# A recurrent attention block with a SwiGLU layer behind it: every engine's order from a list schedule computed in the kernel, fixed tiles, one PSUM pair per role, and the output product accumulated over d_ff

## The chip, the cores and the metric

The kernel runs on one core of a Trainium2 chip. The metric is device time in microseconds (us) of one execution, median of the runs. All matrices are fp32.

## The reference, cut to what matters

```python
for t in range(S):                       # B=4, H=8, S=768, D=40; state is B x H x D x D
    y[:, :, t] = einsum('bhd,bhde->bhe', r_t, state)
    Sa = einsum('bhde,bhe->bhd', state, a_t)
    state = state * w_t[:, :, None, :] - outer(Sa, b_t) + outer(v_t, k_t)
x = y.transpose(0, 2, 1, 3).reshape(3072, 320)
xn = x / sqrt(mean(x * x) + 1e-6) * rms_g
g, val = xn @ w_gate, xn @ w_val         # 320 x 1536 each
out = (g * sigmoid(g) * val) @ w_out     # 1536 x 320
```

The weights `moe_w_gate`, `moe_w_val` and `moe_w_out` arrive as 64-bit floats and are turned into fp32 in the kernel.

## The kernel before, in words

**Chunks.** The 768 steps are cut into 24 chunks of `C = 32`. In each chunk all 32 pairs of batch and head are worked on together, on 128 partitions. A chunk has four parts.

- `front(c)`: loads w, a, k and b of the chunk (`wan`, `kbn`), transposes them (`twa`, `tkb`), and goes through five levels (1, 2, 4, 8, 16). Each level is a Gram product of 32 small matmuls (`gram`), a masked copy of it into `LT` on VectorE (`copy_predicated`, L214), eight transposes (`nat`), a ScalarE copy of these into `KN`, and new `K` and `A`. At the end `LT` goes to DRAM (`sB`) and comes back, spread over the partitions, as `M`.
- `inverse(c)`: 31 pairs of VectorE instructions (`tmp`, L261, and `Yi`, L262), each of which needs the one before; the first needs `M`. The result returns through DRAM (`sY`) into `LT`.
- `crit(c)`: the recurrence over chunks. Matmuls `X` (from `LT`, `VU` and the state `ST`), `U` (needs the inverse), `up`, then the new `ST`; `state()` transposes it (`S`).
- `off(c)`: the chunk's output: transposes of `VU` (`tvu`), `score`, its masked copies `As`, the products `y` (one with the state, five levels), their sums on VectorE, `xn`, the norm, and the transposes `tx` into `xg`.

**Feed-forward.** `feed(g)` works on two chunks (256 rows). For six pairs of 128 columns of d_ff it loads `wf` (320 KB per 128 columns), runs 12 matmuls `h`, then `sg` (a sigmoid on ScalarE) and two VectorE products into `hT`, a tile that holds all 1536 columns. After all of them it loads `wo` twelve times and runs the 24 matmuls `po`. `narrow` turns the weights into fp32 in 48 pieces at the start, with loads and stores on GpSimd's queue.

**What sets the order.** A scheduler outside the kernel orders the instructions by priorities; `together` gives `crit` and `off` a high priority, `feed` raises its three instructions behind `h` by less. Tiles come out of rotating pools, and PSUM is four double banks, `C` for the recurrence, `O` for the output, `B` for `front` and `F` for `feed`.

**Names in the profile.** All matmuls but the transposes stand under L81, the transposes `turned` under L179, all of SP's DMA under L84. Each fp32 matmul appears as two records, a transpose as one.

Of the kernel before, what the change touches and what calls it, by code (L numbers as in the profile page):

```python
# [19 lines left out]
CG = 2  # L20
EPS = 1e-6


@with_exitstack
def kernel(
# [47 lines left out]
    dram = ctx.enter_context(tc.tile_pool(name="dram", bufs=3, space=DRAM))  # L73
    dram1 = ctx.enter_context(tc.tile_pool(name="dram1", bufs=1, space=DRAM))
# [3 lines left out]
    sW = [dram1.tile([P, WF], FP32, name=f"sW{f}") for f in range(FT)]  # L78

    def mm(o, lhsT, rhs, start=True, stop=True):  # L80
        nc.tensor.matmul(o, lhsT, rhs, start=start, stop=stop, skip_group_check=True)  # L81

    def dma(o, i, by=nc.sync):
        by.dma_start(out=o, in_=i)  # L84

    MUL, ADD, SUB = ALU.mult, ALU.add, ALU.subtract
    TT = nc.vector.tensor_tensor
# [8 lines left out]
    def everything():  # L96
        with ExitStack() as st:
            const = st.enter_context(tc.tile_pool(name="const", bufs=1))
            one = st.enter_context(tc.tile_pool(name="one", bufs=1))
            two = st.enter_context(tc.tile_pool(name="two", bufs=2))  # L100
            three = st.enter_context(tc.tile_pool(name="three", bufs=3))
            eight = st.enter_context(tc.tile_pool(name="wf", bufs=4))
            psum = {t: st.enter_context(tc.tile_pool(name="ps" + t, bufs=1, space=PSUM)) for t in "COBF"}

            def dbl(name, tag):
                return psum[tag].tile([P, 2, 512], FP32, name=name, tag=tag)


            ident = const.tile([P, P], FP32, name="ident")
            nc.gpsimd.memset(ident, 0.0)  # L110
            nc.gpsimd.affine_select(ident, ident, pattern=[[-1, P]], channel_multiplier=1, base=0,
                                    compare_op=ALU.not_equal, fill=1.0)

            iw = const.tile([P, 3, C], I32, name="iw")
            nc.gpsimd.iota(iw[:, 0], pattern=[[0, C]], base=0, channel_multiplier=1)
            nc.gpsimd.iota(iw[:, 1], pattern=[[1, C]], base=0, channel_multiplier=0)
            nc.vector.tensor_scalar(iw[:, 0], iw[:, 0], C - 1, None, ALU.bitwise_and)
            TT(iw[:, 0], iw[:, 0], iw[:, 1], ALU.bitwise_xor)
            msk = const.tile([P, len(LEVELS), C], FP32, name="msk")
            for j, l in enumerate(LEVELS):  # L120
                nc.vector.tensor_scalar(iw[:, 2], iw[:, 0], j, None, ALU.logical_shift_right)
                nc.vector.tensor_scalar(msk[:, j], iw[:, 2], 1.0, None, ALU.is_equal)

            mhalf = const.tile([P, 1], FP32, name="mhalf")
            nc.gpsimd.memset(mhalf, -0.5)
            gcol = const.tile([P, KT], FP32, name="gcol")
            for p0, kt, src in ((0, 0, 0), (0, 1, P), (0, 2, 2 * P), (64, 2, 2 * P)):
                m = min(P, DM - src)
                nc.gpsimd.dma_start(out=gcol[p0:p0 + m, kt:kt + 1],
                                    in_=moe_rms_g[src:src + m].rearrange("(d o) -> d o", o=1))  # L130

            eye = const.tile([P, C // 4, C], FP32, name="eye")
            nc.gpsimd.memset(eye, 0.0)
            for m in range(4):
                e = eye[m * BH:(m + 1) * BH]
                nc.gpsimd.affine_select(e, e, pattern=[[-4, C // 4], [1, C]], channel_multiplier=0, base=-m,
                                        compare_op=ALU.not_equal, fill=1.0)


            def keep(shape, name):  # L140
                t = const.tile(shape, FP32, name=name)
                nc.gpsimd.memset(t, 0.0)  # L142
                return t

            kbn_ = [keep([P, N, 2, 64], f"kbn{i}") for i in range(3)]
            wan = keep([P, N, 2, 64], "wan")
            rn = keep([P, N, 2, 64], "rn")
            r2n = keep([P, N, 2, 64], "r2n")
            LT_ = [keep([P, NI, C], f"LT{i}") for i in range(2)]
            VU_ = [keep([P, N, 2, 64], f"VU{i}") for i in range(2)]  # L150
            ST_ = [keep([P, N, 2, 64], f"ST{i}") for i in range(2)]
            nat5 = lambda t: t.rearrange("p n o e -> p (n o) e")

            Z = {}

            def tokens(t, i, x, src, tk):
                dma(nat5(t)[rows(i, x), :, 0:D], src[2 * i:2 * i + 2, :, tk, :].rearrange("q h s d -> s (q h) d"))

            def load(c, *what):
                tk = slice(c * C, (c + 1) * C)  # L160
                for i in range(2):
                    for nm in what:
                        t, x, src = {"k": (kbn_[c % 3], 0, k), "b": (kbn_[c % 3], 1, b), "w": (wan, 0, w),
                                     "a": (wan, 1, a), "v": (VU_[c % 2], 0, v)}[nm]
                        tokens(t, i, x, src, tk)

            def load_r(c):
                tk = slice(c * C, (c + 2) * C)
                for i in range(2):
                    dma(nat5(rn)[half(i), :, 0:D], r[2 * i:2 * i + 2, :, tk, :].rearrange("q h s d -> s (q h) d"))  # L170
                    rv = r[2 * i:2 * i + 2, :, tk, :].rearrange("q (m o) s d -> o s (q m) d", o=2)
                    for o in range(2):
                        dma(r2n[half(o), :, i, 0:D], rv[o])

            def turned(t, name, tag="B"):

                ps = dbl(name, tag).rearrange("p u f -> p (u f)").rearrange("p (n t) -> p n t", n=N)
                for n in range(N):
                    nc.tensor.transpose(ps[:, n, :], t[:, n].rearrange("p o e -> p (o e)"), ident)  # L179
                return ps  # L180

            def front(c):

                z = Z[c] = {}
                if c % 2 == 0:
                    z["rE"] = two.tile([P, N, 2, 2 * C], FP32, name="rE")
                    nc.scalar.copy(z["rE"].rearrange("p n i t -> p n (i t)"), turned(rn, "tr"))
                    z["r2"] = two.tile([P, N, 2, 2 * C], FP32, name="r2")
                    nc.scalar.copy(z["r2"].rearrange("p n o t -> p n (o t)"), turned(r2n, "tr2"))
                else:  # L190
                    z["rE"], z["r2"] = Z[c - 1]["rE"], Z[c - 1]["r2"]
                wa = turned(wan, "twa").rearrange("p n (i x t) -> p (n i) x t", i=2, x=2)
                T = two.tile([P, NI, 2 * C], FP32, name="T")
                z["T"] = Tl = {}
                o = 0
# [372 lines left out]
```

## Time and profile before

| | |
|---|---|
| median of 3 runs | 1994.24 us (1988.46 to 2005.21) |
| profiled execution: time / span | 1989.99 us / 1988.2 us |
| PE busy | 1683.9 us, 85% of the span |
| DVE, ACT, POOL busy | 957.0, 322.2, 299.8 us |
| DMA | 146.25 MB, mean 74 GB/s |
| mean granted TensorE clock | 0.780 |

How to read it: PE's busy time is the sum of records, and a record is longer when the granted clock is lower, so 85% busy does not mean 85% of what PE could do. PEclk in the row of slices is the clock that was granted, in tenths of full speed. The chain of waits names, from the last instruction back, what each step waited for.

### The profile page before, as it was taken

What the parts mean: (1) busy time and instruction counts of PE and PEld (TensorE: products, weight loads), DVE (VectorE), ACT (ScalarE), POOL (GpSimd) and SP (SyncE); (2) the same over time, 40 slices, a digit from 0 to 9 for tenths busy, and PEclk for the clock granted to TensorE, in tenths of its full rate; (3) what the DMA queues carried; (4) which work ended last, traced back from release to release, by engine and by line L of the source; (5) the groups of instructions that cost most, each with busy time, mean ns of one, the idle gap of its engine ahead of it and who ended that gap; (6) DMA issues with size and microseconds to landing.
All of it is one profiled execution on the core that took longest, in us unless ns stands there. A gap on an engine that the chain in (4) does not pass through costs nothing.

```text
span 1988.2 us, 66337 instructions
## 1 busy us (share of the span) xinstructions
PE 1683.9 (85%) x29640; PEld 1303.7 (66%) x29640; DVE 957.0 (48%) x3252; ACT 322.2 (16%) x518; POOL 299.8 (15%) x714
## 2 busy tenths in 40 slices
PE   1748968777899799998898998998998998989886
PEld 1647756666776577666676776776776776767554
DVE  3566566566542543553554525534544544653411
ACT  1111121121111111211211211111211111211100
POOL 4313222122010110110110101101101101110000
PEclk9995575665689877878867678688778688787889
DMA  4333232332333423323423233233233233222232
GB/s 79 70 77 87 68 84 63 79 78 57 101 80 95 84 52 82 79 47 79 87 54 75 62 70 85 60 66 96 66 73 78 60 74 80 62 59 67 66 93 63
DMA packets 309629, 146.25 MB, mean 74 GB/s; under 512 B 262304, under 2 KB 283808, under 8 KB 309344
## 3 DMA queue, kind: packets, MB, share of 16 engines
q1 hardware_dynamic: 303072, 124.31, 27.4%
q0 software_dynamic: 6272, 17.70, 3.1%
q8 instruction: 232, 3.80, 0.8%
q14 instruction: 53, 0.43, 0.1%
HBM read 125.83 MB, written 16.12 MB: 71 GB/s over the span
## 4 chain that ended last, share of the span: by engine, by line
PE 67%; DVE 13%; DMA 8%; issue 5%; ACT 3%; POOL 2%; SPq 1%; POOLq 0%; ACTq 0%; DVEq 0%
PE h L81 19%; PE y L81 11%; PE po L81 9%; PE nat L179 7%; PE gram L81 5%; PE X L81 4%; DMA M<-sB 3%; PE S L179 3%; DVE tmp L261 2%; DVE Yi L262 2%; DVE K L223 2%; PE U L81 2%; DMA rw<-in_moe_w_val_dram 1%; DVE LT L214 1%; PE score L81 1%
## 5 line engine op out<-in xcount | busy, mean ns | idle before, releaser
L81 PE MATMUL h<-xg,wf 128*128 128x256 f32 (+1 forms) x1728 | 506.8, 478 | 36.2 <-issue 19.5
L81 PEld LDWEIGHTS h<-xg,wf 128*128 128x128 f32 (+1 forms) x1728 | 307.1, 227 | 152.3 <-issue 111.7
L81 PE MATMUL po<-wo,hT 128*128 128x320 f32 x576 | 199.2, 492 | 32.8 <-DVE Yi L262 20.1
L81 PEld LDWEIGHTS gram<-A,K 40*64 40x64 f32 x7680 | 161.3, 163 | 98.8 <-issue 47.1
L179 PE MATMUL nat<-ident,K 128*128 128x128 f32 x960 | 190.8, 357 | 36.2 <-DVE LT L214 26.3
L81 PE MATMUL gram<-A,K 40*64 40x16 f32 x7680 | 175.1, 227 | 51.8 <-DVE tmp L261 17.8
L81 PEld LDWEIGHTS y<-As,KN 64*64 64x64 f32 x6144 | 167.6, 170 | 69.6 <-issue 50.3
L261 DVE TENSOR_TENSOR tmp<-Yi,M 128x60 f32<-128x60 f32 (+24 forms) x744 | 166.5, 224 | 93.4 <-DMA M<-sB 80.6
L81 PE MATMUL y<-As,KN 64*64 64x16 f32 x6144 | 193.2, 232 | 18.5 <-issue 14.8
L179 PEld LDWEIGHTS nat<-ident,K 128*128 128x128 f32 x960 | 149.6, 184 | 62.7 <-DVE LT L214 30.9
L262 DVE TENSOR_TENSOR Yi<-Yi,tmp 128x60 f32<-128x60 f32 (+24 forms) x744 | 169.1, 227 | 13.4
L81 PEld LDWEIGHTS po<-wo,hT 128*128 128x128 f32 x576 | 115.4, 214 | 82.5 <-issue 41.6
L246 ACT COPY KN<-nat 128x640 f32<-128x640 f32 x120 | 83.0, 692 | 463.0 <-PE nat L179 463.0
L224 POOL COPY K<-K 128x256 f32<-128x256 f32 x240 | 119.2, 523 | 202.4 <-PE nat L179 88.2
L223 DVE TENSOR_TENSOR K<-K,T 128x256 f32<-128x256 f32 x240 | 117.1, 497 | 39.3 <-PE nat L179 31.5
L433 DVE TENSOR_TENSOR sg<-h,sg 128x512 f32<-128x512 f32 x72 | 49.6, 689 | 168.6 <-ACT sg L432 168.3
L214 DVE COPY_PREDICATED LT<-msk,gram 128x256 f32<-128x256 uint32 x120 | 65.5, 546 | 133.2 <-PE gram L81 132.7
L245 POOL MEMSET KN<- 128x24 f32 x120 | 13.6, 117 | 592.7 <-PE y L81 365.1
L227 POOL COPY A<-A 128x256 f32<-128x256 f32 x120 | 57.7, 481 | 296.8 <-ACT A L201 117.8
L179 PE MATMUL S<-ident,ST 128*128 128x128 f32 x192 | 79.2, 427 | 18.2 <-POOL ST L142 15.2
L432 ACT ACTIVATE sg<-h 128x512 f32<-128x512 f32 x72 | 43.0, 598 | 284.2 <-PE h L81 271.5
L332 DVE TENSOR_TENSOR As<-score,msk 128x256 f32<-128x256 f32 x120 | 42.0, 417 | 65.9 <-PE score L81 65.9
(100 smaller groups left out, 1674.9 us busy)
## 6 DMA issues: line engine op xcount, KB each, us to landing
wf<-sW SPq DMA_DIRECT2D x144, 320.0 KB
wo<-sW SPq DMA_DIRECT2D x144, 160.0 KB
M<-sB SPq DMA_DIRECT2D x24, 512.0 KB
kbn<-in_k_dram SPq DMA_DIRECT2D x48, 80.0 KB
kbn<-in_b_dram SPq DMA_DIRECT2D x48, 80.0 KB
wan<-in_w_dram SPq DMA_DIRECT2D x48, 80.0 KB
wan<-in_a_dram SPq DMA_DIRECT2D x48, 80.0 KB
VU<-in_v_dram SPq DMA_DIRECT2D x48, 80.0 KB
```

The costliest lines, as they stand in the source:

```text
L81: nc.tensor.matmul(o, lhsT, rhs, start=start, stop=stop, skip_group_check=True)
L179: nc.tensor.transpose(ps[:, n, :], t[:, n].rearrange("p o e -> p (o e)"), ident)
L214: nc.vector.copy_predicated(side(LT, l, 1), side(msk, l, 1)[:, j:j + 1].bitcast(U32).to_broadcast((P, NI, G, l)), gr.rearrange("p o n t -> ...
L223: TT(side(K1[:, :, x], l, 0), side(K[:, :, x], l, 0), by[1], MUL)
L224: nc.gpsimd.tensor_copy(side(K1[:, :, x], l, 1), side(K[:, :, x], l, 1))
L227: nc.gpsimd.tensor_copy(side(A1, l, 0), side(A, l, 0))
L246: nc.scalar.copy(t[:, 0:NI * D].rearrange("p (n o e) -> p n o e", n=N, o=2), ps.rearrange("p n (o e) -> p n o e", o=2)[:, :, :, 0:D])
L261: TT(tmp, Y[:, 0:n, i:i + 1].to_broadcast((P, n, m)), M[:, i:i + 1, i + 1:].to_broadcast((P, n, m)), MUL)
L262: TT(Y[:, 0:n, i + 1:], Y[:, 0:n, i + 1:], tmp, SUB)
L332: TT(As[:, j].rearrange("p n (g l) -> p n g l", g=G), side(sc.rearrange("p o n t -> p (o n) t")[:, :, 0:C], l, 1), side(msk, l, 1)[:, j:j ...
L432: nc.scalar.activation(sg, h[:, 0], AF.Sigmoid)
L433: TT(sg, h[:, 0], sg, MUL)
```

## The change

The program is no longer issued as it is described. Each helper (`tt`, `ts`, `where`, `copy`, `scale`, `ptt`, `dma`, `pe`, ...) adds a piece to a `Plan`: the engine, a due time, an assumed duration, and the tiles that it reads and writes. At the end `Plan.issue` goes through all engines by a list schedule (at the earliest time at which some engine has a ready piece, that engine takes the ready piece that is due first) and issues the pieces in that order under `tc.manual_schedule()`, so that nothing reorders them.

```diff
+class Plan:
+    LATENCY = 0.1
...
+            t, e = best
+            i = min((i for i in waiting[e] if ready[i] <= t), key=lambda i: (self.pieces[i][1], i))
+            waiting[e].remove(i)
+            _, _, time, more, _ = self.pieces[i]
+            free[e] = t + time
+            order.append((t, i))
+            for j in users[i]:
+                ready[j] = max(ready[j], t + time + more + self.LATENCY)
...
+        for _, i in sorted(order):
+            self.pieces[i][4]()
...
+    def tt(due, o, a, b, op):
+        plan.add("DVE", due, 0.145 + 0.00104 * size(o), lambda: nc.vector.tensor_tensor(o, a, b, op), [o], [a, b])
+    def copy(due, o, a):
+        plan.add("ACT", due, 0.16 + 0.00083 * size(o), lambda: nc.scalar.copy(o, a), [o], [a])
+    def dma(due, o, i, by="SP"):
+        q, t = {"SP": (nc.sync, 0.06), "POOL": (nc.gpsimd, 1.0)}[by]
+        n = size(i) * list(i.ap)[0][1]
+        plan.add(by, due, t, lambda: q.dma_start(out=o, in_=i), [o], [i], 2.2 + n * 4 / 200e3)
...
+    ps_ = {t: Turns(n, [P, 2, 512], "ps" + t, pool=psum) for t, n in (("C", 1), ("B", 1), ("H", 1), ("O", 1))}
...
+        due = d + T - 8                      # front(c), d = (c - 2) * T, T = 46.0
+        for i in range(2):
+            dma(due, sB[i * NI:(i + 1) * NI].rearrange("n (s t) -> s n t", s=C), LT[rows(i, 1)])
+        dma(due, M.rearrange("p s t -> p (s t)"), bass.AP(sB.tensor, sB.offset, [[0, 4], [C * C, BH], [1, C * C]]))
...
+            tt(d + i, tmp, ...)              # inverse(c), d = (c - 1) * T + 4
+            tt(d + i, Y[:, 0:n, i + 1:], Y[:, 0:n, i + 1:], tmp, SUB)
...
+                dma(d - 20, wf[e], sW[f + e])            # feed: gate, value and output weights in one tile
+                pe(d + 2 * e, 2.2, [mm(h[:, q, e], ...) ...])
+            act(d + 4, sg, h[:, 0], AF.Sigmoid)
+            tt(d + 4, sg, h[:, 0], sg, MUL)
+            tt(d + 5, hT, h[:, 1], sg, MUL)
+            for e in range(2):
+                pe(d + 9 + e, 1.1, [mm(po[:, q, 0:DM], hT[:, e, q * P:(q + 1) * P], wf[e][:, 5 * P:],
+                                       f + e == 0, f + e == FT - 1) for q in range(CG)])
```

Beside the order, these things change.

- **Tiles** are fixed (`Turns`), each with its count of buffers: one `wan`, three `LT`, one `M`, three of each `KN`, five `wf` (`WB`). `KN`'s padding is zeroed once.
- **PSUM.** One double bank per role: `C` for the recurrence and the output together, `B` for `front`, `H` for `h`, `O` for `po`.
- **Output product.** `po` runs behind each pair of `h` and accumulates over d_ff for the whole of `feed`; `hT` holds one pair, and `wf` brings the 160 KB of output weights along (480 KB per 128 columns, 144 loads instead of 288).
- **Engines.** The copies of half of `K` go from POOL to ACT, the product for `A` and `Sdec` from DVE to POOL, the second halves of `Xs` and `VU`, and the scaling of `x`, from DVE to ACT; at levels 1 and 16 one DVE instruction makes both halves of `K`.
- **Others.** The transposes of r (`rn`, `r2n`) move from `front` into the main part of even chunks. `narrow` works in 24 pieces of 480 columns through `wf`, `sg` and `hT`, with seven DVE instructions each instead of eight, and its DMA is on SP's queue.

The first place is on PE: `S`, the transposes of the new state, and the products `y`, in a chunk in the second half of the program. Before:

```order
L81 MATMUL y_16146<-r_13588,Sd 64x32 x32
L81 MATMUL y_16146<-As,KN_14906 64x16 x32
L81 MATMUL y_16146<-As,KN_14835 64x16 x24
L179 MATMUL S<-ident,ST_160 128x128
L81 MATMUL y_16146<-As,KN_14835 64x16
L179 MATMUL S<-ident,ST_160 128x128
L81 MATMUL y_16146<-As,KN_14835 64x16
L179 MATMUL S<-ident,ST_160 128x128
L81 MATMUL y_16146<-As,KN_14835 64x16
```

Of the change (`psC` holds the recurrence and the output, `psB` the front, `psH` h, `psO` po):

```order
L225 MATMUL psC_222<-ident,ST_134 128x128 x8
L222 MATMUL psO_225<-wf_208,hT_216 128x320 x2
L222 MATMUL psC_222<-rE_193,vut_197 64x32 x32
L222 MATMUL psB_223<-A_183,K_180 64x16 x32
L222 MATMUL psH_224<-xg_206,wf_209 128x256 x6
L222 MATMUL psC_222<-r_194,Sd_173 64x32 x32
L225 MATMUL psB_223<-ident,K_180 128x128 x8
L222 MATMUL psC_222<-As_198,KN_1_162 64x16 x32
L222 MATMUL psH_224<-xg_206,wf_210 128x256 x6
L222 MATMUL psC_222<-As_198,KN_1_156 64x16 x32
```

Every block of matmuls now stands whole, the eight transposes of the state ahead of `score`, and between the small blocks stand blocks of `h`, `po` and transposes. Before, single transposes alternate with single matmuls of `y`.

The second place is on DVE: the last masked copy into `LT` of a chunk (`COPY_PREDICATED` 128x16x16), and the first instruction of `inverse` that needs `M` (`tmp` 128x31). Before:

```order
L433 TENSOR_TENSOR sg<-h,sg 128x512
L214 COPY_PREDICATED LT_152<-msk,gram 128x16x16
L434 TENSOR_TENSOR hT<-h,sg 128x512
L299 COPY VU_158<-U 32x2x8x40
L332 TENSOR_TENSOR As<-score,msk 128x256 x5
L307 TENSOR_TENSOR ST_160<-up,Sdec 128x2x8x40
L433 TENSOR_TENSOR sg<-h,sg 128x512
L302 TENSOR_TENSOR Sdec<-ST_160,T 128x640
L434 TENSOR_TENSOR hT<-h,sg 128x512
L261 TENSOR_TENSOR tmp<-Yi,M 128x31
```

Of the change, in an even chunk:

```order
L195 COPY_PREDICATED LT_137<-msk,psB_223 128x16x16
L183 TENSOR_TENSOR y_199<-y_199,T_178 128x32x8
L183 TENSOR_TENSOR y_199<-y_199,psC_222 128x8x2x8 x2
L183 TENSOR_TENSOR y_199<-y_199,T_178 128x64x4
L183 TENSOR_TENSOR y_199<-y_199,psC_222 128x8x4x4 x2
L183 TENSOR_TENSOR y_199<-y_199,T_178 128x128x2
L183 TENSOR_TENSOR y_199<-y_199,psC_222 128x8x8x2 x2
L183 TENSOR_TENSOR tmp_191<-Yi_189,M_188 128x31
L183 TENSOR_TENSOR y_199<-y_199,T_178 128x256
L183 TENSOR_TENSOR Yi_189<-Yi_189,tmp_191 128x31
L183 TENSOR_TENSOR y_199<-y_199,psC_222 128x2x8x16
```

Between the two stood the instructions of `hT`, `VU`, `As`, `ST` and `Sdec`; now there are nine short sums of `y`, and the last two sums of `y`, which `xn` needs, stand behind `tmp`. In odd chunks more stands between, among it all sums of `y`.

More of the change, by code (lines that the diff above doesn't have):

```diff
@@ new lines, with turned, tokens @@
+    col = lambda n: slice(n * D, (n + 1) * D)
+    flat = lambda t: t.rearrange("p n o e -> p (n o) e")
+    Z = {}
+    def turned(due, t, tag):
+        ps = ps_[tag].next().rearrange("p u f -> p (u f)").rearrange("p (n t) -> p n t", n=N)
+        pe(due, 0.95, [flip(ps[:, n, :], t[:, n].rearrange("p o e -> p (o e)"), ident) for n in range(N)])
+        return ps
+    def tokens(due, t, i, x, src, tk):
+        dma(due, flat(t)[rows(i, x), :, 0:D], src[2 * i:2 * i + 2, :, tk, :].rearrange("q h s d -> s (q h) d"))
@@ L541 @@
+    for c in range(-2, NCH):
+        if c >= 0:
+            main(c)
+            if c % CG == CG - 1:
+                feed(c // CG)
+        if c + 2 < NCH:
+            front(c + 2)
+            inverse(c + 2)
+    with tc.manual_schedule():
+        plan.issue()
 _INS = ['r', 'k', 'v', 'w', 'a', 'b', 'moe_w_gate', 'moe_w_val', 'moe_w_out', 'moe_rms_g']
```

804 lines of the change are left out of this document (405 added, 399 removed).

## The prediction

> **What bounds the kernel now.** I read the page first, then the chain of waits for the pace of the chunks, then the stretches and the timeline at the places where PE is slow.
>
> ```profile
> span 1988.2 us, 66337 instructions
> PE 1683.9 (85%) x29640; PEld 1303.7 (66%) x29640; DVE 957.0 (48%) x3252; ACT 322.2 (16%) x518; POOL 299.8 (15%) x714
> PE   1748968777899799998898998998998998989886
> PEclk9995575665689877878867678688778688787889
> PE 67%; DVE 13%; DMA 8%; issue 5%; ACT 3%; POOL 2%; SPq 1%; POOLq 0%; ACTq 0%; DVEq 0%
> ```
>
> PE holds the chain for 67%, and no other engine is half busy. But the granted clock moves between 0.5 and 0.9 slice by slice, so PE's time is not a fixed sum. The starts of product X in the chain give the pace:
>
> ```profile
> 160.59 3.61 PE X L81 x128
> 220.51 3.50 PE X L81 x128
> 1396.01 3.50 PE X L81 x128
> 1541.55 3.50 PE X L81 x128
> 1828.11 3.50 PE X L81 x128
> ```
>
> 220.51 is chunk 2, 1828.11 the last, chunk 23: 21 chunks in 1607.6 us, 76.6 each; in the second half two chunks take 145.5, 72.8 each. Behind the last X come 160 us. Now that pair, and stretches with their granted clock (columns: stretch, its length, busy time of PE, of weight loads, DVE, ACT and POOL with records, PEclk, DMA share, GB/s):
>
> ```profile
> 1396.00:1541.55 145.55, 133.12 (x2473) 102.47 (x2474) 71.72 (x243) 25.05 (x39) 17.89 (x46) 0.80 0.31 74
> 857.00:884.25 27.25, 27.25 (x403) 19.69 (x402) 11.80 (x47) 3.48 (x7) 0.90 (x4) 0.50 0.12 29
> 604.50:662.40 57.90, 51.29 (x597) 36.70 (x595) 12.20 (x30) 11.33 (x16) 3.79 (x9) 1.00 0.43 107
> 955.95:959.35 3.40, 1.99 (x16) 1.52 (x15) 2.42 (x12) 1.64 (x4) 0.42 (x1) 1.00 0.78 176
> 959.40:962.70 3.30, 1.24 (x6) 1.06 (x6) 3.23 (x13) 0.81 (x1) 0.76 (x2) 1.00 0.08 11
> 1495.30:1502.05 6.75, 5.93 (x16) 4.42 (x17) 5.16 (x19) 0.69 (x1) 1.01 (x2) 0.50 0.09 25
> ```
>
> The clock is 1.00 or 0.50, and PE's being busy does not decide it: 27.25 of 27.25 us busy at half, 51.29 of 57.90 busy at full. What is run decides. The slow stretch holds small matmuls and single transposes, the fast one long runs of h and po.
>
> In the pair, the clock of 0.80 grants 0.80 x 145.55 = 116 us of full speed; of that some 11 go with the 12.4 us in which PE is idle. So **PE's work is 105 us at full clock, 52.5 per chunk**. Of the 72.8 us per chunk, 6.2 are idle and some 14 are lost to half clock.
>
> **The change: PE's work.** No matmul is added or removed. At full clock:
>
> ```profile
> 606.53 1.09 PE L179 MATMUL nat<-ident,K 128*128 128x128 f32 x8
> 609.31 5.18 PE L81 MATMUL h<-xg,wf 128*128 128x256 f32 x24
> 614.42 0.52 PE L81 MATMUL gram<-A,K 40*64 40x16 f32 x18
> 622.10 1.12 PE L81 MATMUL gram<-A,K 40*64 40x16 f32 x64
> 624.64 3.40 PE L81 MATMUL po<-wo,hT 128*128 128x320 f32 x12
> 627.87 0.38 PE L179 MATMUL nat<-ident,K 128*128 128x128 f32 x2
> ```
>
> A pair of h blocks takes 614.42 - 609.31 = 5.11, its po (8 of these records) 8/12 x 3.23 = 2.15, so 21.8 per chunk with three pairs. The 28 smaller blocks of a chunk show about 1.1 with a tail of some 0.15 under the next, so 27 together: 49, which agrees with the 52.5 less what interleaving costs. That is here:
>
> ```profile
> 857.00 0.47 PE L179 MATMUL S<-ident,ST 128*128 128x128 f32 x1
> 857.41 0.39 PE L81 MATMUL y<-As,KN 64*64 64x16 f32 x2
> 857.73 0.47 PE L179 MATMUL S<-ident,ST 128*128 128x128 f32 x1
> ```
>
> At half clock one transpose and one y take 0.73, eight pairs 5.8; whole blocks would take about 2.2 at half. The change puts them whole, so I take off 2.5 at full clock: **50 us per chunk** (bounds 48 and 52.5).
>
> **The added wait.** `tmp`, the first use of M, now stands close behind the last masked copy, in DVE's fixed order. The times of that path, by SP's and DVE's timeline:
>
> ```profile
> 1324.03 0.97 SPq L84 DMA_DIRECT2D sB<-LT  x2
> 1328.33 0.57 SPq L84 DMA_DIRECT2D M<-sB  x1
> 1338.80 0.19 DVE L261 TENSOR_TENSOR tmp<-Yi,M 128x31 f32<-128x31 f32 x1 [0.47 <-DMA M<-sB]
> ```
>
> 14.8 us from the store to the first use, where `dma` in the change assumes two transfers of 2.5 and 4.8. With hops and the copy ahead M is there some 15.5 us after the last gram block. In even chunks PE has po, two nat, three y, po, h and twa in its order from there to `xn`: 2.15 + 2 x 0.95 + 3 x 0.95 + 2.56 + 0.95 = 10.4. `xn` needs the last two sums of y, which are queued behind `tmp`, so PE stands for 15.5 - 10.4 + 1 = 6. In odd chunks the next X needs PSUM that the copy to `xg` frees, and that is queued behind six instructions of the inverse: 18 against 13.4 us of blocks, so 4.6. Mean **5.5 per chunk**. Below this it can be nothing, if other waits have pulled the two apart already; above it 15, if nothing covers it.
>
> Shorter waits: a round trip over ACT (tvu after tr2 with one gram between, U after X) exceeds its cover by some 0.5 us at four or five places: **2** (bounds 0 and 5).
>
> **Half clock after it.** Idle of this size is followed by half clock: the last row of the stretches is 6.75 us at 0.50 (it follows a wait of DVE for PE's pair), the longest spell 27. In the new order a block of h or po stands at about every third row, so I take 9 us per spell and 1.2 spells per chunk: half of 11 us is lost, **5.5** (bounds 0 and 14, as now).
>
> Pace: 50 + 5.5 + 2 + 5.5 = **63 us**.
>
> **Start and end.** The first front now runs at half clock as before:
>
> ```profile
> 43.82 1.97 PE L179 MATMUL twa<-ident,wan 128*128 128x128 f32 x8 [4.54 <-ACT r L189]
> 69.03 1.91 PE L81 MATMUL gram<-A,K 40*64 40x16 f32 x64 [0.87 <-ACT KN L246]
> ```
>
> 27 us from twa to the last gram, now from about 8 us (an estimate: the loads of w and a are first in SP's queue, and the transposes of r are moved off it). So 35, M at 50, and the inverse, 62 instructions among those of `narrow`, some 55 us: U at 111 with its trip through DRAM. Chunks 0 and 1 have no feed-forward, stay at half clock, and take 47 to 60 each (59.9 from X of chunk 1 to that of 2 above). X of chunk 2 at **205** (200 to 230; before 220.51). `narrow`'s DVE work is less (seven instructions instead of eight) and beside it.
>
> At the end the last feed runs alone. Before:
>
> ```profile
> 1936.53 5.16 PE L81 MATMUL h<-xg,wf 128*128 128x256 f32 x24 [2.20 <-issue]
> 1943.88 5.15 PE L81 MATMUL h<-xg,wf 128*128 128x256 f32 x24 [2.19 <-issue]
> 1967.56 14.16 PE L81 MATMUL po<-wo,hT 128*128 128x320 f32 x48 [2.24 <-DVE hT L434]
> ```
>
> A pair takes 7.35 with a gap of 2.2, and po 14.2 behind all. Now po (2.15) fits in the gaps: 6 x 7.35 = 44, one po pair, the copy and the output 9: **53**.
>
> **Moved and hidden.** Rows for what moves engine:
>
> ```profile
> L224 POOL COPY K<-K 128x256 f32<-128x256 f32 x240 | 119.2, 523 | 202.4 <-PE nat L179 88.2 <-ACT K L203 54.4 <-DVE Yi L262 23.7
> L396 POOL TENSOR_TENSOR ss<-ss,mhalf 128x1 f32<-128x1 f32 x24 | 13.4, 557 | 198.7 <-DVE ss L395 198.7
> L302 DVE TENSOR_TENSOR Sdec<-ST,T 128x640 f32<-128x640 f32 x24 | 19.7, 823 | 0.4
> ```
>
> A POOL product of 256 isn't in the trace: between 0.5 (the copy) and 1.1 (with the 0.557 of one element on top); five per chunk, levels 7 us apart, so hidden at either end. `Sdec` on POOL, 0.8 to 1.9, has U and up for cover. ACT goes from 25.05 in the pair to some 40, of 126. Without the cover, the copies of K would cost 5 x 0.7 per chunk. SP's queue gets `narrow`'s DMA in the start alone; the wf loads wait there as they do now. Nothing of these is in the sum.
>
> **Sum:** 205 + 22 x 63 + 53 = 1644, and 1.8 around the span (1989.99 against 1988.2): 1646. The profiled run is 4 us under the median, so **1650**.
>
> **Rivals.**
>
> - *A. Dense work keeps the clock full.* No half spells but behind the start: 205 + 22 x 57.5 + 53 + 6 = 1529. For it: 1.00 over 57.9 us of h, po, gram and nat above. Against: in that stretch PE never stood long. 0.24. The Trainium skill, "TensorE: Matmul & The Clock Gate", Part 1, says that sustained PE activity of about 3.4 us releases the throttle and only idle time brings it back. By this rule A would hold; but the stretch at 857.00 is busy throughout at 0.50, so this trace speaks against the rule as it stands.
> - *B. The clock stays at 0.80.* The waits of DVE and PE scatter, and each chunk spends 40% at half. Then 57.5 / 0.80 = 72: 205 + 22 x 72 + 53 + 6 = 1848. For it: such waits start most spells now. Against: h was bunched in runs of up to 24 before, and is now spread. 0.19. The same page, Part 4, says that transposes do not count as busy for the gate; then ten blocks per chunk would not hold it, and B would follow. But in 955.95 to 959.35 nothing but the blocks below ran, and the stretch behind it is at 1.00: the trace disagrees.
>
> ```profile
> 955.75 1.09 PE L179 MATMUL twa<-ident,wan 128*128 128x128 f32 x8
> 958.01 1.09 PE L179 MATMUL tkb<-ident,kbn 128*128 128x128 f32 x8 [1.16 <-ACT A L201]
> ```
>
> - *C. Slower: M's load waits on SP behind a wf load.*
>
> ```profile
> SPq L84 <- PE h L81: 469.0, 99, 19.8
> ```
>
> Such waits of SP reach 19.8 us now. If one stood ahead of M in each chunk, PE would stand 17 us longer, with two half windows more: 80 or above, 205 + 22 x 81 + 53 = 2040. It decides from about 80 per chunk. Against: the wf load ahead of M waits for a po that stands one row after the last gram block. 0.06.
> - *D. The change doesn't do what it says* (waits keep the engines in the old step): no change, 1994, 0.04. The order shows the new places, so little.
>
> **How the numbers follow.** Forecast (60 to 66 per chunk) 0.47, A 0.24, B 0.19, C 0.06, D 0.04. The range takes A nearly whole and B: pace 55.5 with X of chunk 2 at 200 gives 1480, pace 72.8 gives 1860. Within 1% is what a measurement of this kernel can hardly tell from no change. Faster: forecast, A and B, 0.90; same: D, 0.04; slower: C, 0.06.
>
> **What would show it.** X of chunk 2 near 205, then every 63 us; S in whole blocks; DVE's wait for M at `tmp` of some 5 us in each chunk and PE's behind it at `xn` or X; a mean clock of 0.88 to 0.93; po in the gaps of h at the end. The forecast is wrong if M comes much sooner or later than 15 us, if the clock stays at 0.80 or goes to 1.00, or if waits other than M's fill over 5 us per chunk.

## The result, and the profile after

The changed kernel takes 1675.05 us (median of four runs, 1660.15 to 1681.0), the kernel before 1991.35 in the same session: ratio 0.843, 95% interval 0.834 to 0.852. The forecast was 1650, its range 1480 to 1860. The profiled execution took 1676.31 us. From its page:

```profile
span 1674.5 us, 65373 instructions
PE 1370.3 (82%) x29632; PEld 1095.6 (65%) x29632; DVE 859.4 (51%) x2767; ACT 444.0 (27%) x805; POOL 202.1 (12%) x360
PEclk9997559797998998998998989999989989989878
PE 64%; DMA 17%; DVE 8%; issue 5%; ACT 4%; SPq 2%; POOL 0%; DVEq 0%; ACTq 0%; POOLq 0%
```

PE is busy for 314 us less (1683.9 before) with practically the same count of records. That can only be the length of records, and PEclk shows why: behind the start it is 0.7 to 0.9, where it was 0.5 to 0.9. The DMA share of the chain has doubled, from 8 to 17%. Product X (now `psC<-VU,LT`) gives the pace, by PE's timeline (chunks 2 and 23):

```profile
261.15 1.36 PE L222 MATMUL psC<-VU,LT 32*32 32x40 f32 x64
1567.94 1.36 PE L222 MATMUL psC<-VU,LT 32*32 32x40 f32 x64 [0.72 <-DVE xg L183]
```

So X of chunk 2 comes at 261, then 21 chunks take 1306.8 us, **62.2 each**, and 106.6 us lie behind the last X. Between these two marks the stretch of the kernel before and that of the change read as follows (columns as in the prediction):

```profile
220.51:1828.11 1607.60, 1424.45 (x25830) 1103.45 (x25832) 793.76 (x2715) 272.06 (x434) 227.74 (x556) 0.76 0.31 73
```

```profile
104.20:261.10 156.90, 103.23 (x2378) 92.87 (x2374) 97.61 (x320) 41.58 (x78) 22.54 (x35) 0.67 0.40 98
261.10:1567.90 1306.80, 1140.68 (x25481) 903.41 (x25479) 666.42 (x2200) 364.82 (x659) 153.02 (x274) 0.91 0.39 85
```

I split the pace of every kernel in one way. Idle is length less PE's busy time. The trace records the granted clock as 1.00 or 0.50 at every moment, so half of PE's busy time at 0.50 is lost to half clock, and the rest of the busy time is work at full clock. ((1 - PEclk) times the length, which the rows give by themselves, would count idle time at 0.50 as lost too: 18.4 us per chunk before, 5.6 after.) Before: 76.6 = 8.7 idle + 16.5 half clock + 51.3 work. After: 62.2 = 7.9 + 4.1 + 50.2. **Of 14.3 us won per chunk 12.4 are clock**, and the idle time has hardly changed. Executions of one kernel differ in their clock: the kernel before has 0.780 over the whole of this profile and 0.79 to 0.81 in its later executions, at nearly the same times. So differences of about 1 us between two kernels' half clock are not resolved.

The waits after, with PE's part in it:

```profile
DVE tmp L183 <- DMA M<-sB: 141.4, 23, 9.8
PE psH L222 <- DVE xg L183: 70.3, 10, 9.2
PE psC L222 <- DVE y L183: 50.0, 17, 5.9
```

DVE waits 6.1 us per chunk for M, and PE behind it: in odd chunks 7 us for `xg`, in even ones some 4 for `y`, from which `xn` is made (the 17 waits for `y` hold short ones too). Over all 23 chunks that is 5.2 us of PE per chunk. One of each in the timeline:

```profile
1173.16 0.84 SPq L219 DMA_DIRECT2D sB<-LT  x2
1175.51 0.56 SPq L219 DMA_DIRECT2D M<-sB  x1
1186.66 0.19 DVE L183 TENSOR_TENSOR tmp<-Yi,M 128x31 f32<-128x31 f32 x1 [5.11 <-DMA M<-sB]
1187.70 0.68 PE L222 MATMUL psC<-ident,y 40*64 40x40 f32 x32 [3.94 <-DVE y L183]
1188.31 4.26 PE L222 MATMUL psH<-xg,wf 128*128 128x256 f32 x12
...
1254.93 4.94 PE L222 MATMUL psH<-xg,wf 128*128 128x256 f32 x12 [5.56 <-DVE xg L183]
```

M is there 13.5 us after the store was issued, 11.2 of them for the load alone. The last two sums of `y` stand behind `tmp` in DVE's fixed order and come with it. Behind either wait the next block of h takes 4.3 to 4.9 us instead of 2.6: half clock.

### The profile page after: what moved, and what is told of

It reads as the page before. It is cut to its first block, busy times and chain, and to the rows that moved or that the text cites. A ratio compares the mean times of both kernels' runs of the same rounds, so it can differ in the third digit from the quotient of the medians.

```text
span 1674.5 us, 65373 instructions
## 1 busy us (share of the span) xinstructions
PE 1370.3 (82%) x29632; PEld 1095.6 (65%) x29632; DVE 859.4 (51%) x2767; ACT 444.0 (27%) x805; POOL 202.1 (12%) x360
## 4 chain that ended last, share of the span: by engine, by line
PE 64%; DMA 17%; DVE 8%; issue 5%; ACT 4%; SPq 2%; POOL 0%; DVEq 0%; ACTq 0%; POOLq 0%
PE psH L222 23%; PE psC L222 16%; DMA M<-sB 14%; PE psO L222 9%; PE psB L225 8%; PE psB L222 4%; PE psC L225 4%; SPq L219 2%; DMA sB<-LT 1%; DVE y L183 1%; DVE hT L183 1%; ACT Xs L202 1%; ACT K L198 1%; DMA kbn<-in_b_dram 1%; DVE Yi L183 1%
## 5 line engine op out<-in xcount | busy, mean ns | idle before, releaser
L222 PE MATMUL psH<-xg,wf 128*128 128x256 f32 (+1 forms) x1728 | 425.3, 441 | 70.3 <-DVE xg L183 70.3
L222 PEld LDWEIGHTS psH<-xg,wf 128*128 128x128 f32 (+1 forms) x1728 | 285.6, 210 | 168.3 <-DVE xg L183 71.7
L183 DVE TENSOR_TENSOR tmp<-Yi,M 128x60 f32<-128x60 f32 (+24 forms) x744 | 174.9, 235 | 157.5 <-DMA M<-sB 141.4
L222 PE MATMUL psO<-wf,hT 128*128 128x320 f32 x576 | 202.3, 477 | 22.2 <-DVE hT L183 21.8
L183 DVE TENSOR_TENSOR Yi<-Yi,tmp 128x60 f32<-128x60 f32 (+24 forms) x744 | 189.0, 254 | 17.3
L222 PE MATMUL psB<-A,K 40*64 40x16 f32 x7680 | 150.7, 217 | 36.3 <-ACT K L198 20.7
L222 PEld LDWEIGHTS psB<-A,K 40*64 40x64 f32 x7680 | 139.9, 150 | 61.2 <-issue 30.8
L225 PE MATMUL psB<-ident,K 128*128 128x128 f32 x960 | 153.2, 311 | 27.8 <-DVE LT L195 23.4
L225 PEld LDWEIGHTS psB<-ident,K 128*128 128x128 f32 x960 | 125.5, 160 | 37.9 <-DVE LT L195 24.4
L222 PEld LDWEIGHTS psO<-wf,hT 128*128 128x128 f32 x576 | 104.3, 201 | 58.1 <-DVE hT L183 25.3
L222 PEld LDWEIGHTS psC<-As,KN 64*64 64x64 f32 x6144 | 109.4, 147 | 26.1 <-issue 24.6
L222 PE MATMUL psC<-As,KN 64*64 64x16 f32 x6144 | 117.8, 216 | 8.1 <-issue 3.9
```

What stands on the lines that cost most here:

```text
L183: plan.add("DVE", due, 0.145 + 0.00104 * size(o), lambda: nc.vector.tensor_tensor(o, a, b, op), [o], [a, b])
L222: return o, lhsT, rhs, lambda: nc.tensor.matmul(o, lhsT, rhs, start=start, stop=stop, skip_group_check=True)
L225: return o, i, ident, lambda: nc.tensor.transpose(o, i, ident)
```

## The experiments

Ratios are to the kernel before, run in the same session. The table gives the split between X of chunk 2 and X of chunk 23; a kernel's row of the view by stretches is quoted where a verdict rests on it.

| kernel | time, us | ratio (95% interval) | X of chunk 2 | pace | idle | half clock | work |
|---|---|---|---|---|---|---|---|
| before | 1991 | 1 | 220.5 | 76.6 | 8.7 | 16.5 | 51.3 |
| changed | 1675 | 0.843 (0.834 to 0.852) | 261 | 62.2 | 7.9 | 4.1 | 50.2 |
| before, S whole | 1902 | 0.956 (0.950 to 0.961) | 210 | 71.7 | 9.7 | 12.2 | 49.8 |
| list schedule undone | 1951 | 0.980 (0.975 to 0.985) | 275 | 74.5 | 10.4 | 14.9 | 49.2 |
| feed bunched | 1810 | 0.909 (0.903 to 0.915) | 256 | 68.9 | 10.6 | 9.2 | 49.1 |
| longer assumed load | 1670 | 0.836 (0.827 to 0.845) | 253 | 62.0 | 6.9 | 5.6 | 49.5 |
| fill in odd chunks | 1760 | 0.884 (0.878 to 0.889) | 257 | 65.7 | 7.8 | 5.7 | 52.1 |
| an eighth of M | 1534 | 0.770 (0.766 to 0.774) | 245 | 56.2 | 2.9 | 3.1 | 50.2 |
| M in two parts | 1589 | 0.804 (0.797 to 0.811) | 248 | 58.6 | 4.4 | 4.2 | 50.1 |
| two parts, 4 `kbn` | 1525 | 0.770 (0.765 to 0.775) | 253 | 55.4 | 2.8 | 2.4 | 50.3 |

**The list schedule undone.** The pieces in the order of the program; the outer scheduler sets each engine's order.

```diff
-    with tc.manual_schedule():
-        plan.issue()
+    for p in plan.pieces:
+        p[4]()
```

> The changed kernel with the same tiles, the same PSUM per role, the same engines and the output product accumulated over d_ff, but the pieces are issued in the order in which the program makes them, and the outer scheduler sets each engine's order, as in the kernel before. Theory (the order by due times is what moves the pace): most of the gain is gone, 1880 to 2000 us, a pace of 70 us or more per chunk. Rival (the tiles, the whole blocks of S and the product in the gaps of h bring it): 1650 to 1760 us, a pace below 66.

1950.94 us. X of chunk 2 comes 54 us later than before, since the first loads now stand behind those of the weights:

```profile
PE psB L225 <- DMA wan<-in_a_dram: 94.5, 2, 88.0
```

So the pace decides, and it is 74.5, as the theory has it. Half clock is back at 14.9 us per chunk, from 4.1; idle is up by 2.5 only. Three stretches of 50 us, first all, then the busy time of `psH` (h) alone:

```profile
1300.00:1350.00 50.00, 44.65 (x549) 32.79 (x548) 22.42 (x83) 12.21 (x23) 4.04 (x8) 0.88 0.35 89
1350.00:1400.00 50.00, 45.34 (x868) 37.93 (x866) 13.78 (x33) 9.59 (x18) 4.83 (x9) 0.76 0.39 91
1400.00:1450.00 50.00, 38.83 (x1062) 35.26 (x1060) 26.82 (x100) 14.08 (x27) 6.89 (x12) 0.60 0.19 34
```

```profile
1300.00:1350.00 50.00, 22.63 (x96) 15.69 (x96) 5.50 (x8) 2.39 (x4) 0.88 0.35 89
1350.00:1400.00 50.00, 10.16 (x48) 7.12 (x48) 2.79 (x4) 1.20 (x2) 0.76 0.39 91
1400.00:1450.00 50.00, 0.00 (x0) 0.00 (x0) 0.00 (x0) 0.00 (x0) 0.60 0.19 34
```

PE is about as busy in the second stretch as in the first; the clock goes with the h in it (the third has more idle time as well). Same tiles, same PSUM, same accumulation over d_ff: without the order they bring 2% here, 54 us of a later start included.

**The feed bunched.** The other way round: the list schedule stays, and h and po are pressed into every second chunk.

```diff
-        per = CG * T / (FT / 2)
+        per = CG * T / (FT / 2) / 2
```

> The changed kernel with the feed's due times pressed into half of the distance: its h and po blocks stand in the even chunk alone, the odd chunk has only the small blocks and transposes. The same work. Theory (what PE runs sets the clock: h and po spread through every chunk are what keeps it at 1.00): the odd chunks fall to a mean clock of 0.5 to 0.7, the even ones stay at 0.9 to 1.0; time lost to half clock goes from 4 us per chunk back to 10 or more, the time to 1800 to 1950 us. Rival 1 (the list schedule's short waits alone keep the clock): half clock stays at 4 to 6 us, the time at 1700 or below. Rival 2 (the odd chunk without feed is bound by waits instead): PE's idle time doubles, from 7.8 to 15 us per chunk, at an unchanged share of half clock.

1809.6 us, as the theory has it. An odd chunk between two even ones:

```profile
956.90:1027.40 70.50, 63.41 (x1105) 48.68 (x1103) 27.43 (x87) 16.17 (x26) 4.75 (x8) 0.93 0.50 113
1027.40:1099.60 72.20, 54.90 (x1370) 47.17 (x1370) 38.71 (x140) 19.06 (x39) 11.35 (x20) 0.67 0.19 38
1099.60:1168.00 68.40, 63.03 (x1105) 48.52 (x1103) 24.56 (x75) 16.18 (x26) 4.76 (x8) 0.95 0.52 116
```

The chunk without h and po takes as long as those with them, at a clock of 0.67. Idle went up as well (17.3 of 72.2 us there), so this does not separate lack of dense work from idle time entirely; but half clock rose by 5.1 us per chunk, idle by 2.7.

**S whole, in the kernel before.** One part of the change alone.

```diff
-                    Sd[c + 1] = state(c + 1)
+                    with tc.high_priority(offset=9000):
+                        Sd[c + 1] = state(c + 1)
```

> The kernel before, with one part of the change alone: the eight transposes of the next S are emitted as one block instead of singly between the products y. Theory (the term of 2.5 us of full clock per chunk in the prediction's sum): 23 x 2.5 = 58 us less, with half clock on part of it up to 85 less: 1905 to 1935 us. Rival 1 (PE then waits where the transposes had filled gaps between the y): 1970 to 1995, no change. Rival 2 (the clock rises as well, since the single transposes and y's were the worst stretches for it): 1880 or below, with a mean clock above 0.82.

1902.11 us, 84 less than before: within the 85 that the theory allowed, 3 us below the range of times that it gave. The mean clock is 0.827 in the profile (0.808 to 0.827 in the four executions), around the 0.82 that rival 2 named, at a time that rival 2 did not reach. Of 4.9 us per chunk, 4.3 are half clock and 1.6 are work; idle went up by 0.9. So the clock rose as well, as rival 2 had it, by less.

**M at a fixed order.** Each engine keeps its order row for row, a clear of M at the start apart; the load brings an eighth, so the inverse is not that of the reference.

```diff
-        dma(due, M.rearrange("p s t -> p (s t)"), bass.AP(sB.tensor, sB.offset, [[0, 4], [C * C, BH], [1, C * C]]))
+        Mf, few = M.rearrange("p s t -> p (s t)"), 4 * C
+        plan.add("SP", due, 0.06, lambda: nc.sync.dma_start(
+            out=Mf[:, 0:few], in_=bass.AP(sB.tensor, sB.offset, [[0, 4], [C * C, BH], [1, few]])),
+                 [Mf], [bass.AP(sB.tensor, sB.offset, [[0, 4], [C * C, BH], [1, C * C]])], 2.2 + P * C * C * 4 / 200e3)
```

> The changed kernel with every engine's order unchanged row for row; the load of M moves an eighth of its bytes (4 of its 32 rows; the rest stays zero, so the inverse is not that of the reference). The plan goes on assuming the whole load. Theory (at this order the wait for M is what PE's waits for `xg` and y come from, 5.2 us per chunk in the profile): DVE's wait at `tmp` falls from 6.1 to under 1.5 us per chunk, PE's idle time from 7.8 to 3 or 4, half clock falls with it by 1 to 3 us per chunk, the pace to 54 to 57, the time to 1500 to 1565 us. Rival (as with the longer assumed time, another wait comes in its place: xn for x, U for LT): the wait at `tmp` falls but PE's idle time stays above 6 us, the pace at 60 or more, the time at 1630 or more.

1534.05 us, the theory. The wait and the steady stretch:

```profile
DVE tmp L183 <- DMA M<-sB: 2.4, 4, 0.9
```

```profile
245.00:1424.90 1179.90, 1118.76 (x25483) 887.00 (x25481) 669.61 (x2200) 364.41 (x659) 153.71 (x274) 0.94 0.37 87
```

141.4 us of DVE's waiting are down to 2.4, PE's idle time falls by 5.0 per chunk and half clock by 1.1 (hardly more than executions differ); the pace falls by 6.0. At this order **the wait for M costs 141 us** (1675 to 1534); of 143 between the two profiles' spans 16 are in the start and 127 in the 21 chunks. Idle time is not the whole of the half clock, though: 3.1 of 4.1 us stay when M's wait is gone. The Trainium skill, "TensorE: Matmul & The Clock Gate", Part 1, names idle time of about 3.4 us as what brings the throttle back; this trace shows falls after less: 30 of its 32 falls from 1.00 to 0.50 had no idle gap of PE of 3.4 us anywhere in the 6.8 us before them.

**The plan told of the slow load.** The load gets 7 us more in the plan, so `tmp` stands later.

```diff
-        plan.add(by, due, t, lambda: q.dma_start(out=o, in_=i), [o], [i], 2.2 + n * 4 / 200e3)
+        plan.add(by, due, t, lambda: q.dma_start(out=o, in_=i), [o], [i], 2.2 + n * 4 / 200e3 + late)     # late=7.0 for M
```

> The changed kernel, with the plan's assumed time of the load of M longer by 7 us (M was assumed there 4.8 us after its store; the profile shows 10 to 12 us for the load). The list schedule then sets `tmp` some 20 rows of DVE behind the last masked copy instead of 7 to 14. Theory (the wait for M costs PE 5 to 6 us per chunk, and half clock behind it): DVE's wait at `tmp` falls from 6.1 us per chunk to under 2, the pace from 62.2 to 53 to 57 us, the time to 1500 to 1580 us. Rival (the wait only moves: what hangs on `tmp`, the last y, xn and the next X, comes as late as before, and PE stands there): the wait at `tmp` falls, but the pace stays at 60 or more, and the time at 1630 or more.

1670.22 us: the rival. DVE's wait for M is 3.6 us in the whole program, but:

```profile
PE psC L225 <- ACT x L202: 71.3, 10, 9.8
PE psB L225 <- DMA kbn<-in_b_dram: 36.9, 11, 7.2
```

```profile
1127.49 0.40 POOL L214 COPY Yi<-eye 128x256 f32<-128x256 f32 x1 [36.45 <-DMA sY<-Yi]
...
1128.64 0.55 POOL L211 TENSOR_TENSOR ss<-ss,mhalf 128x1 f32<-128x1 f32 x1
```

With the inverse later, its store is later, POOL's copy into `Yi` waits for that store, and the norm's power (`ss`) is queued behind the copy. PE waits for `x` as long as it had waited for `xg` (71.3 and 70.3 us).

**That queue, and the conversions.** The kernel with the longer assumed load, the copy into `Yi` on DVE, and `narrow` due later (next).

```diff
-        pcopy(d, Y, eye)
+        plan.add("DVE", d, 0.43, lambda: nc.vector.tensor_copy(Y, eye), [Y], [eye])
```

> The changed kernel with the longer assumed load of M, the later `narrow`, and the copy of the unit matrix into Yi on DVE instead of POOL. With the longer assumed load alone, that copy stood on POOL up to 36 us waiting for the store of sY, and the power for `ss` behind it came late, so that PE waited 71 us in all for x in the odd chunks. Theory (that queue on POOL is what took the place of the wait for M): PE's waits for x go from 71 to under 20 us, its idle time from 6.9 to 3.5 us per chunk, the pace from 62.0 to 55 to 58, the time to 1500 to 1580 us. Rival (the next wait stands right behind, kbn's load or LT): pace 60 or more, and only the start's gain is seen, 1620 to 1660 us.

1705.65 us, X of chunk 2 at 295, pace 62.3: the rival in its pace, and worse than it in time, by the start. DVE now waits for the store itself (89.2 us), and PE still waits 70.2 us for `x`. My naming of POOL's queue as the cause fell. The store's lateness stands at both waits; a kernel with the store alone earlier was not run.

**Fill.**

```diff
+            pe(d + 40.5, 5.1, [mm(fill, x[:, 0:P], row) for _ in range(12)])    # odd chunks, ahead of tx
```

> The changed kernel, with 12 matmuls more (128x256, 2.6 us at half clock for 6 of them, 5.1 us for all at full clock, a result that nothing reads) in each odd chunk, placed right before the transposes tx, next to which PE stands waiting for DVE's `xg`. It is 61 us more of PE's work over 12 feeds. Theory (idle PE is what starts the spells of half clock, and the stall of the odd chunks is idle): the fill lies in the idle time and keeps the clock up, so the time stays at 1676 or falls to as little as 1630, and the mean clock of the steady part goes from 0.91 to 0.94 or more. Rival (the spells start elsewhere, or what PE runs decides and the stall is not where it is lost): the time goes up by 30 to 61 us, to 1706 to 1737, at a clock of 0.91.

1760.44 us, 85 more than the change: beyond the rival even.

```profile
PE psC L225 <- ACT x L202: 34.5, 5, 8.3
PE psH L222 <- DVE xg L183: 34.4, 7, 7.9
PE psB L225 <- DMA kbn<-in_b_dram: 29.8, 6, 7.9
```

The wait for `xg` is half of what it was, those for `x` (9.3 us in the change) and `kbn` (4.5) have taken its place, idle stays at 7.8, and half clock goes from 4.1 to 5.7. The fill did not raise the clock. Its matmuls also changed the list schedule's order, so how much of the 85 us is the fill itself stays open.

**M in two parts.** Step i of the inverse reads row i of M alone, so the first 8 rows come first, the other 24 in a second tile; all engines' order but SP's stays.

```diff
+            nc.sync.dma_start(out=M[0].rearrange("p s t -> p (s t)"), in_=part_(0, few))                # few = 8 * C
+            nc.sync.dma_start(out=M[1].rearrange("p s t -> p (s t)"), in_=part_(few, C * C - few))
```

> The changed kernel, every engine's order unchanged but for one DMA more per chunk: M is loaded in two parts, first the 8 rows that the first 8 steps of the inverse read, then the other 24, into a tile of their own. Nothing is left out. Theory (the wait at the first `tmp` is for the bytes of the whole load, and later rows are needed later): as with the eighth of the load, the first part lands some 7 us sooner and the rest is there when step 8 comes, so DVE's wait for M falls under 2 us per chunk, the pace to 56 to 57.5, the time to 1530 to 1570 us. Rival (the second part shares the DMA engines with the first, so the first comes no sooner, or step 8 waits for the second): the wait for M stays at 4 us or more per chunk in all, and the time at 1630 or more.

1589.45 us, 0.804: the theory's mechanism, 19 us above its range. One load in the timeline, and the waits:

```profile
1057.89 0.56 SPq L401 DMA_DIRECT2D M<-sB  x1
1058.49 0.56 SPq L402 DMA_DIRECT2D M<-sB  x1
1063.15 0.19 DVE L183 TENSOR_TENSOR tmp<-Yi,M 128x31 f32<-128x31 f32 x1 [2.44 <-DMA M<-sB]
```

```profile
DVE tmp L183 <- DMA M<-sB: 15.5, 12, 2.4
PE psB L225 <- DMA kbn<-in_b_dram: 34.0, 13, 6.7
```

The first part is there after 5.3 us instead of 11.2. The largest wait beyond those with the eighth of M is PE's for `kbn` (8.1 us there): 26 of the 55 us between the two.

**And a fourth `kbn`.** Its load waited for a buffer that the last product of the chunk before still read.

```diff
-    kbn = Turns(3, [P, N, 2, 64], "kbn", True)
+    kbn = Turns(4, [P, N, 2, 64], "kbn", True)
```

> The kernel with M loaded in two parts, and a fourth buffer for kbn, so that its load no longer waits for the last product y of the chunk before and stands earlier on SP; the list schedule's order moves in places. Theory (with M in two parts PE waited 34 us in all for the load of kbn, which comes right behind the second part): that wait falls below 12 us, the pace from 58.5 to 56 or 57.5, the time from 1589 to 1540 to 1570. Rival (the new order brings another wait, as the longer assumed load of M did): pace 58 or more, 1580 or more.

**1525.39 us, 0.770 of the kernel before**, 9% below the change, with all of the work done: the fastest of this study, and 15 us below what was expected.

```profile
PE psB L225 <- DMA kbn<-in_b_dram: 11.6, 1, 11.6
DVE tmp L183 <- DMA M<-sB: 7.6, 8, 1.8
```

```profile
252.60:1416.60 1164.00, 1105.84 (x25483) 879.28 (x25481) 668.98 (x2200) 364.50 (x659) 154.78 (x274) 0.96 0.41 95
```

PE is busy for 95% of the stretch at 0.96, which is what rival A had asked for; here it took the end of two waits for DMA, not dense work alone.

**The start, three times.** First `narrow` due later:

```diff
-        d = -T + 8 * f
+        d = 10 * f
```

> The changed kernel with the due times of `narrow` (conversion of the weights) from 0 to 110 instead of from -46 to 42, so that the list schedule sets its 168 DVE instructions behind those of the first fronts and inverses wherever both are ready. Theory (the start came out 56 us longer than forecast since DVE, with the conversions in its order, kept PE waiting for LT and As): product X of chunk 2 comes at 205 to 235 us instead of 261, the pace stays at 62, the time falls by 25 to 55 us, to 1620 to 1650. Rival (PE at half clock and the round trips through DRAM set the start, or the conversions then delay the first wf): X of chunk 2 stays within 10 us of 261, or the first feed waits, and the time is 1665 or more.

1682.11 us, X of chunk 2 at 271: the rival. Then `narrow` without its arithmetic (the lines from `ex` to the last product, but for one):

```diff
-        ts(d, ex, hi, 20, 0x7ff, ...)
         ts(d, mt, hi, 0xfffff, None, ALU.bitwise_and)
-        act(d, m, mt, ...)
...
```

> The changed kernel with seven of the eight instructions of `narrow` left out (six of the seven on DVE, the one on ACT; what is stored as weights is then not the weights), its DMAs kept. Theory (the conversions that stand between the steps of the first inverses in DVE's order are what makes the start 56 us longer than forecast; the inverse of chunk 1 takes 63 us there): 24 x 6 x 0.5 = 72 us less of DVE, and X of chunk 2 at 200 to 220 us instead of 261; the pace stays at 62; the time 1615 to 1640. Rival (the half clock of PE, the round trips through DRAM and the load of M set the start): X of chunk 2 at 245 or later, the time 1660 or more.

1660.95 us, X of chunk 2 at 255, which is the rival by its bound, but not for its reason: chunk 0 starts only at 140, since the list schedule now puts a third front ahead of it, and the first two chunks take 115 us instead of 157 from X to X. So the order had to be held:

```diff
-        ts(d, ex, hi, 20, 0x7ff, ALU.logical_shift_right, ALU.bitwise_and)
+        small(V.tensor_scalar, "DVE", ex, [hi, 20, 0x7ff], dve, ...)     # issued on 16 columns, planned as 480
```

> The changed kernel with every engine's order unchanged row for row (two clears of `sg` and `hT` at the start apart): the instructions of `narrow` work on 16 columns instead of 480, so that each takes some 0.2 us instead of 0.4 to 0.65 (what is stored as weights is not the weights); the plan goes on assuming them whole. Leaving them out had changed the order: a third front stood ahead of X of chunk 0, and what the first two chunks gained (115 us instead of 147 from U to U) went there. Theory (at this order the conversions are what makes the first two chunks long): the inverse of chunk 1 falls from 63 us to 40 or less, the two chunks to 115 to 130 us, X of chunk 2 comes at 225 to 245 instead of 261, the time is 1640 to 1662. Rival (ACT's round trip, the stores of sW and half clock set them): the inverse of chunk 1 stays over 52 us, X of chunk 2 at 252 or later, the time 1664 or more.

1655.18 us, X of chunk 2 at 248. The first `tmp` and the last `Yi` of chunk 1's inverse, as changed and with thin conversions:

```profile
117.40 0.41 DVE L183 TENSOR_TENSOR tmp<-Yi,M 128x31 f32<-128x31 f32 x1
180.10 0.17 DVE L183 TENSOR_TENSOR Yi<-Yi,tmp 128x8 f32<-128x8 f32 x1
```

```profile
112.85 0.18 DVE L183 TENSOR_TENSOR tmp<-Yi,M 128x31 f32<-128x31 f32 x1
167.02 0.17 DVE L183 TENSOR_TENSOR Yi<-Yi,tmp 128x8 f32<-128x8 f32 x1
```

62.9 us become 54.3. This lies between the two: the time is in the theory's range, X of chunk 2 is 3 us above it, and the inverse stays over the rival's 52. The conversions' length explains 13 of the 56 us by which the forecast's start was too short (261 to 248). The steps of that inverse stand between those of chunk 0 and of a front, at a clock of 0.67; what each of these adds was not separated. In the kernel before the same inverse took some 40 us (first `tmp` at 133.4, last at 173.5).

## Why the prediction was right, by its steps

By the sum: forecast 205 + 22 x 63 + 53 = 1644; measured 261 + 22 x 62.2 + 44.4 = 1674.

- **Pace, 63: 62.2.** And by its terms: idle 5.5 + 2 = 7.5 (7.9), work 50 (50.2), half clock 5.5 (4.1). The rivals' paces, 57.5, 72 and 81, are all further off.
- **S, 2.5 at full clock.** Right in its place, wrong in kind. The rows that I read give 5.8 - 2.2 = 3.6 us at half clock, 1.8 at full; with no row for the rest I took off 2.5, from 52.5. The pair that I read has 52.7 by the clock's record, but the mean over all chunks is 51.3, so the change took off 1.1 and the 50 was met with the help of a pair above the mean. S alone brought 4.9 us per chunk, most of it clock.
- **The wait for M.** Forecast: M 15.5 us behind the last gram, PE standing 5.5. DVE's wait is 6.1, PE's 5.2, and M comes 13.5 us after its store. The mean was met by two halves that miss in opposite ways: some 4 us for 6 in even chunks, 7 for 4.6 in odd ones (the two forecasts' mean is 5.3, which I rounded up to 5.5). PE's place in the odd chunks was named wrongly: not the next X for its PSUM, but the first h of the next feed, one row ahead, which reads `xg` itself. With the wait taken away at a fixed order the pace fell by 6.0.
- **Half clock, from a block of h or po at every third row.** Forecast: 1.2 spells per chunk of 9 us, half of it lost. The clock's record has 1.43 spells of 8.2 us, from 2.57 of 14.2 before; PE was idle for 3.5 of the 11.7 us, so 4.1 are lost. Shown by both directions: undone order 14.9, bunched feed 9.2, spread feed 4.1. By size it is nearly the whole gain, but the spread of h and po is not all of it: S whole took off 4.3 in the kernel before, and bunching the feed gave back 5.1.
- **The start, 205: 261. This is the step that failed**, mis-sized by 56 us. U of chunk 0 came at 121 instead of 111, and from there to X of chunk 2 it took 140 us instead of 94 (in the kernel before 87: U at 133.9, X of chunk 2 at 220.5). I took the length of the first chunks from the kernel before. In the fixed order the inverse of chunk 1 stands between `narrow`, a front and the chunk at hand and takes 63 us, where it had taken 40. I had the conversions as "beside it"; their length is 13 of the 56 us, the rest was not separated.
- **The end, 53: 44.4, by two errors that cancel.** From the chain:

```profile
1602.41 8.17 PE psH L222 x24
...
1614.05 2.36 PE psH L222 x12
1616.41 1.27 PE psO L222 x4
...
1621.44 0.70 DVE hT L183
1622.19 2.44 PE psO L222 x4
1624.63 2.95 PE psH L222 x12
```

  A pair takes 10.6 us (1614.05 to 1624.63; others 10.1), not 7.35: po stands beside h, not in the gap, which is still there between h's end and `hT`. But the last chunk, with nothing beside it, took 34.5 us instead of a pace of 63 (X at 1567.94, the last feed from 1602.41).
- **POOL's product of 256**, bounded by 0.5 and 1.1, takes 0.751 us (96 of them, 72.0 us) and is hidden, as forecast.

So the sum of 1644 is 30 us below the span of 1674.5: a start too short by 56, less 18 for the pace and 9 for the end. The forecast came as near as 25 because errors of both signs met; its pace is right by its terms.

## What to carry to other kernels

When a trace shows PE busy and its clock at half, ask which blocks follow each other: blocks kept whole, with dense work spread evenly among small matmuls and transposes, were worth 12.4 us of 76.6 per chunk here, without a matmul less. A list schedule is as good as its assumed durations, but correcting one of them moves the wait rather than removing it; what helped was to shorten the transfer itself (load first what is read first) and to free a buffer sooner. And to price one wait in a planned kernel, shrink the work while the plan still assumes it whole: if the order changes too, the ablation answers another question, as leaving `narrow` out did.

## What the runs showed of the hardware

M's load, 512 KB that read the same 128 KB four times, is there 11.2 us after its issue in the timeline above. A load of `wf` of nearly the same size lands in a third of that, by the changed kernel's view of DMA (count, KB of one, median us from issue to landing):

```profile
wf<-sW SPq DMA_DIRECT2D x144, 480.0 KB, 3.8
```

The packets show why. M's 128 packets of 4096 bytes move four at a time: for 77% of the time in which any is under way exactly four are, while those of `wf` reach 16 at once. In the kernel before, a stretch in which next to nothing but M's packets ran has a quarter of the 16 DMA engines busy; in the change the loads that are issued behind M join it, the engines are full, and M's packets take 282 ns instead of 159 (medians). First a stretch of the kernel before, then two of the change:

```profile
1334.00:1337.00 3.00, 3.00 (x20) 2.21 (x18) 0.09 (x1) 0.60 (x1) 0.00 (x0) 1.00 0.25 80
```

```profile
1178.00:1180.00 2.00, 2.00 (x68) 1.40 (x67) 0.00 (x0) 0.00 (x0) 0.00 (x0) 1.00 0.19 70
1181.00:1186.60 5.60, 2.77 (x18) 1.79 (x16) 0.51 (x3) 0.00 (x0) 0.00 (x0) 1.00 1.06 167
```

The access pattern of M's load has 4 as its outermost count. That this is what holds it to four was not tested; no load with another outer count was run.

The second surprise is the clock, counted over the whole traces in steps of 3.41 us, of which every spell within them is a multiple. A fall to 0.50 comes after a step with idle time: before, the steps ahead of the 59 falls were 57% busy (median), in the change those ahead of 38 falls 43%, and none of these 38 was over 90% busy (10 of the 59 were). But PE's being busy does not end a spell. In the kernel before 130 steps at 0.50 were over 95% busy, and the next one was at 0.50 as well; small matmuls filled half of such a step (median). In the 58 steps after which the clock rose they filled 3% (mean), and h, po and transposes nearly all the rest. The change has 18 of the first kind and 37 of the second (4%). In the kernel with the list schedule undone 13 of 47 rises came after steps that transposes alone filled to over 90%. So the kernel before idles 8.7 us per chunk at a clock of 0.76 and the change 7.9 at 0.91: what differs most is how soon a dense block ends a spell. This is a count of what stood next to what; no run changed the kind of the blocks alone.
